# One decode step of attention plus an MLP mixer: TensorE's whole program in loops, V always in one home of SBUF

## The chip, the cores and the metric

The kernel runs on one core of a Trainium2 chip. A core has five engines with instruction streams of their own: PE (TensorE, matrix products into PSUM), DVE (VectorE), ACT (ScalarE), POOL (GpSimd) and SP (SyncE, which here issues nearly all loads). Each engine has a sequencer that reads instructions, works out addresses held in registers, takes branches, waits on semaphores, and hands the rest to its engine; PE's sequencer is called PEldq or PEq in the profile. Sixteen DMA engines move data between HBM and the on-chip memory SBUF. The metric is the device time in microseconds (us) of one execution; lower is better.

## What is computed

Two branches work on one token x of 1024 values, and their results are added. The attention has 32 query heads on 4 heads of K and V, with 65,536 cached keys of 128 values each: 64 MB of K and 64 MB of V in bf16.

```python
def _A_ref(x, k_cache, v_cache, wq, wo):          # Hq 32, Hkv 4, Sk 65536, Dh 128
    q = (x @ wq).reshape(B, Sq, Hq, Dh)            # transposed to b h s d
    scores = einsum("bhqd,bhkd->bhqk", q, k) * Dh ** -0.5
    o = einsum("bhqk,bhkd->bhqd", softmax(scores), v)
    return o.reshape(B, Sq, Hq * Dh) @ wo

def _B_ref(x, w1, w2, w3, w4):                     # S = 1, D 1024, F 3584
    h = gelu(layernorm(x) @ w1)
    # four quarters of h are shifted by 1, -1, 2, -2 tokens, with zeros let in
    x1 = x + shifted(h) @ w2
    return x1 + gelu(layernorm(x1) @ w3) @ w4

xn = layernorm(A_x)
return A_x + _A_ref(xn, ...) + _B_ref(xn, ...)
```

With one token, every shifted value is a zero that was let in, so the product with w2 adds nothing, though both kernels still load w1 and w2 and multiply by them.

## The kernel before

**Tiles.** Each head of K and V is cut into two tiles of 32,768 keys (r = 0 and 1), so there are 8 tiles (g, r), each with a K load and a V load of 8.39 MB. A tile of K or V fills a whole slot; there are three slots in SBUF, and the weights pass through the same slots. The list `items` (L193 to L201) is the order of the loads: wq, K(0,0), V(0,0), w3, K(0,1), V(0,1), wa (w1 and half of w4), then K and V in turn, wb (the rest of w4, and w2) ahead of the last V, and wo. Item i goes into slot i mod 3, and wo into the slot of the last K (L208, L209).

**Order.** Nothing schedules the work: the class `Flow` (L22) keeps for every buffer who wrote and read it, and puts a `wait_ge` on an engine's queue ahead of the instruction that needs it. Each engine runs in the order of the text. SP's loads are issued by `load` (L211): item i + 3 after the work on item i has been written down (L571), so a load waits on SP until the last user of its slot is done, and all later loads wait behind it.

**A tile of K** (`compute_K`, L442): DVE transposes the slot in place in four quarters (L449). PE multiplies each quarter by the queries into the scores `sc` in PSUM, in a hardware loop (`Fori`, L452) over the four banks; for most tiles the loop's body takes two quarters, 8 matmuls (CGS = 2), for the last tile one quarter, 4 matmuls (n_cg, L443). Its first matmul starts the accumulation. DVE takes the maximum (L462), two small transpositions on PE and two small steps on DVE give the common maximum (L463 to L469), ACT exponentiates all scores into `work` (L471), and DVE transposes `work` (L473).

**A tile of V** (`compute_V`, L495): 64 matmuls, written out one by one, four column groups side by side (L503). For r = 0 ACT copies the result to `ob` (L509), for r = 1 `group_end` (L513) adds both halves on DVE, and one matmul and four small DVE steps bring the group's output into `oT`.

**Weights.** `rows_product` (L314) multiplies the token by wq, w3 and w1, with the output row in four pieces on four column groups of PE at once. `rows_loop` (L328) does w4, w2 and the first 10 rows of wo with hardware loops; the other pieces of wo are written out (L536) and end the kernel, before a copy (L560) and the output's DMA.

Of the kernel before, what the change touches and what calls it, by code (L numbers as in the profile page):

```python
# [16 lines left out]
WO_PIECES = (10, 10, 8, 3, 1)  # L17
WO_UNROLL = 5
CGS = 2


class Flow:  # L22


    def __init__(self, nc, ctx):
        self.nc = nc
        self.ctx = ctx
        self.engines = {"T": nc.tensor, "V": nc.vector, "S": nc.scalar, "G": nc.gpsimd, "Q": nc.sync}
        self.sems = {}
        self.counts = {}  # L30
        self.seen = {e: {} for e in self.engines}
        self.writer = {}
        self.readers = {}

    def sem(self, name):
        if name not in self.sems:
            self.sems[name] = self.ctx.enter_context(self.nc.semaphore(f"s_{name}"))
            self.counts[name] = 0
        return self.sems[name]

    def _wait(self, eng, reads, writes):
# [7 lines left out]
        for key in reads:  # L49
            if key in self.writer:  # L50
                token = self.writer[key]
                if token[0] != "T" or eng != "T":
                    add(token)
        for key in writes:
            if key in self.writer:
                token = self.writer[key]
                if token[0] != "T" or eng != "T":
                    add(token)
            for token in self.readers.get(key, ()):
                if token[0] != eng:  # L60
                    add(token)
        for name, value in need.items():
            if self.seen[eng].get(name, 0) < value:
                self.engines[eng].wait_ge(self.sem(name), value)
                self.seen[eng][name] = value
# [8 lines left out]
    def op(self, eng, reads, writes, emit, times=1):  # L74

        self._wait(eng, reads, writes)
        sem = self.sem(eng)

        def signal(ins):
            ins.then_inc(sem, 1)  # L80

        emit(signal)
        self.counts[eng] += times
        self._note((eng, self.counts[eng]), reads, writes)
# [7 lines left out]

    def one(self, eng, reads, writes, call):
        self.op(eng, reads, writes, lambda signal: signal(call(self.engines[eng])))
# [3 lines left out]
def kernel(  # L98
# [28 lines left out]
    assert S == 1 and DH == P and REP == 8 and HQ == 32 and DC == 8 and NOUT == 1024  # L127
# [4 lines left out]
    FW = F // 8  # L132
    assert FW <= 512 and F % 8 == 0 and FW % 16 == 0 and FW // 16 == FC and OC == 32
    NQ = NOUT // 4
    NH = NOUT // 2
    FH = FC // 2
# [9 lines left out]
    slots = [tile_sb([P, KEYS], BF16, f"slot{i}") for i in range(SLOTS)]  # L146
    work = tile_sb([P, HF * 512], BF16, "work")
    ob = tile_sb([P, 512], F32, "ob")
    xpad = tile_sb([P, DC, 32], BF16, "xpad")
    QS = P + 24  # L150
    qst = [tile_sb([P, 4, QS], BF16, f"qst{i}") for i in range(2)]
    qsel = tile_sb([P, 4, HQ], BF16, "qsel")
    ident_bf = tile_sb([P, P], BF16, "ident_bf")
    ident_f = tile_sb([P, P], F32, "ident_f")
    og = tile_sb([P, P + 1], F32, "og")
    msk = tile_sb([P, 4, 32], F32, "msk")
    hstrip = tile_sb([P, 192], BF16, "hstrip")
    gsel = tile_sb([P, P], BF16, "gsel")
    sel32 = tile_sb([P, 32], F32, "sel32")
    sel8 = tile_sb([P, 8], F32, "sel8")  # L160
    sel8x = tile_sb([P, 32], F32, "sel8x")
    mask16 = tile_sb([P, 16], F32, "mask16")
    mask64 = tile_sb([P, 64], F32, "mask64")
# [3 lines left out]
    lnb = tile_sb([P, 8, DC], F32, "lnb")  # L167
    x_bf = tile_sb([P, DC], BF16, "x_bf")
    xn2b = tile_sb([P, DC], BF16, "xn2b")
    qT = tile_sb([P, HQ], BF16, "qT")  # L170
    hf_f = tile_sb([P, FC], F32, "hf_f")
    hT = tile_sb([P, FC], BF16, "hT")
    gT = tile_sb([P, DC], BF16, "gT")
    o5 = tile_sb([P, 32], F32, "o5")
    oT = tile_sb([P, OC], BF16, "oT")
    rep = msk[0:1].rearrange("p a b -> p (a b)")

    sc = ps.tile([P, HF, 512], F32, name="sc")
    oacc = ps.tile([P, 512], F32, name="oacc")
    pm = ps.tile([P, 512], F32, name="pm")  # L180
    psR = ps.tile([P, 2, 512], F32, name="psR")
    psB = sc[:, 0, :]
# [7 lines left out]
    assert sum(WO_PIECES) == OC  # L190
    wo_start = [sum(WO_PIECES[:i]) for i in range(len(WO_PIECES))]

    items = [("wq",), ("K", 0, 0), ("V", 0, 0), ("w3",)]  # L193
    for g in range(HKV):
        for r in range(NT):
            if (g, r) != (0, 0):
                items += [("K", g, r), ("V", g, r)]
            if (g, r) == (0, 1):
                items += [("wa",)]
    items.insert(len(items) - 1, ("wb",))  # L200
    items += [("wo",)]  # L201
# [4 lines left out]
    one, op = fl.one, fl.op  # L206

    slot_of = [i % SLOTS for i in range(len(items))]  # L208
    slot_of[-1] = slot_of[items.index(("K", HKV - 1, NT - 1))]  # L209

    def load(i):  # L211
        item, s = items[i], slot_of[i]
        t, kind = slots[s], items[i][0]
# [4 lines left out]
        elif kind == "wa":  # L218
            loads = [(0, w1_v), (KEYS // 2, w4_v[:, 0:FH * NOUT])]
        elif kind == "wb":  # L220
            loads = [(0, w4_v[:, FH * NOUT:FC * NOUT]), (KEYS // 2, w2_v)]
# [3 lines left out]
        else:  # L225
            cache = A_k_cache if kind == "K" else A_v_cache
            _, g, r = item
            loads = [(0, cache[0, g, r * KEYS:(r + 1) * KEYS, :].rearrange("(p k) d -> p (k d)", p=P))]
        fl._wait("Q", [], [("slot", s), ("slot", s, 1)] + [("slot", s, q) for q in range(2, 5)] + [("kt", s, cg) for cg in range(4)])
        for n, (at, src) in enumerate(loads):  # L230
            key = ("slot", s) if n == 0 else ("slot", s, n)
            fl.dma("Q", f"slot{s}" if n == 0 else f"slot{s}_{n}", [], [key], t[:, at:at + src.shape[-1]], src)

    qrow = work[:, 0:1024].rearrange("p (b n) -> p b n", b=2)
    psel = work[:, 1024:1536].rearrange("p (b m) -> p b m", b=4)
    ones_f = og[:, 0:P]
    xr = work[:, 1536:2048]

    load(0)
    fl.dma("S", "x", [], ["x_bf"], x_bf[:], A_x[0, 0, :].rearrange("(p c) -> p c", c=DC))  # L240
    load(1)
    load(2)
    one("G", [], ["xr"], lambda e: e.memset(xr[0:33, :], 0.0))
    fl.dma("S", "x2", [], ["xr"], xr[0:33:32, :], A_x[0, 0, :].rearrange("(j n) -> j n", j=2))

    def ident(t, key):
        one("G", [], [key], lambda e: e.memset(t[:], 0.0))
        one("G", [key], [key], lambda e: e.affine_select(
            out=t[:], in_=t[:], compare_op=ALU.not_equal, fill=1.0, base=0, pattern=[[-1, P]],
            channel_multiplier=1))  # L250

    eps_t, negmean, rstd, ln_s1, ln_s2 = (sm[:, i:i + 1] for i in range(5))
    ident(ident_bf, "ident_bf")
    ident(ident_f, "ident_f")
    one("G", [], ["eps"], lambda e: e.memset(eps_t, LN_EPS))
    one("G", [], ["ones"], lambda e: e.memset(ones_f, 1.0))
    one("G", [], ["xpad"], lambda e: e.memset(xpad[:], 0.0))
    one("G", [], [("qst", 0)], lambda e: e.memset(qst[0][:], 0.0))
    one("G", [], [("qst", 1)], lambda e: e.memset(qst[1][:], 0.0))
    one("G", [], ["hstrip"], lambda e: e.memset(hstrip[:], 0.0))  # L260

    def v(reads, writes, call):
        one("V", reads, writes, call)

    v(["ident_f"], ["sel32"], lambda e: e.tensor_tensor(out=sel32[:], in0=ident_f[:, 0:32], in1=ident_f[:, 32:64], op=ALU.add))
    v(["ident_f", "sel32"], ["sel32"], lambda e: e.tensor_tensor(out=sel32[:], in0=sel32[:], in1=ident_f[:, 64:96], op=ALU.add))
    v(["ident_f", "sel32"], ["sel32"], lambda e: e.tensor_tensor(out=sel32[:], in0=sel32[:], in1=ident_f[:, 96:128], op=ALU.add))
    v(["sel32"], ["mask16"], lambda e: e.tensor_tensor(out=mask16[:], in0=sel32[:, 0:16], in1=sel32[:, 16:32], op=ALU.add))
    v(["ident_f"], ["mask64"], lambda e: e.tensor_tensor(out=mask64[:], in0=ident_f[:, 0:64], in1=ident_f[:, 64:128], op=ALU.add))
    v(["sel32"], ["dmask"], lambda e: e.reduce_sum(out=dmask[:], in_=sel32[:].rearrange("p (cg h) -> p cg h", h=8), axis=AX.X))  # L270
    v(["sel32"], ["mask4"], lambda e: e.reduce_sum(out=mask4[:], in_=sel32[:].rearrange("p (x dd) -> p dd x", dd=4), axis=AX.X))
    v(["sel32"], ["sel8"], lambda e: e.reduce_sum(out=sel8[:], in_=sel32[:].rearrange("p (cg h) -> p h cg", h=8), axis=AX.X))
    v(["sel8"], ["sel8x"], lambda e: e.tensor_copy(out=sel8x[:].rearrange("p (h dd) -> p h dd", dd=4),
                                                   in_=sel8[:].unsqueeze(2).to_broadcast([P, 8, 4])))
    iv = ident_bf[:].rearrange("p (b i r) -> p b r i", b=2, r=2)
    for b in range(2):
        for par in range(2):
            v(["ident_bf"], [("psel", b, par)], lambda e: e.tensor_copy(
                out=psel[:, 2 * b + par, :].rearrange("p (a i) -> p a i", a=4),
                in_=iv[:, b, par, :].unsqueeze(1).to_broadcast([P, 4, 32])))  # L280
    psel_keys = [("psel", b, par) for b in range(2) for par in range(2)]
    lead = ident_bf[:].rearrange("p (j u) -> p j u", u=32)[:, :, 0]
    v(["ident_bf", "hstrip"], ["hstrip"], lambda e: e.tensor_copy(
# [322 lines left out]
```

## Time and profile before

| what | value |
|---|---|
| median of 3 runs | 402.4 us (402.27 to 402.55) |
| the profiled execution's own time | 402.23 us |
| its span, first to last instruction | 400.1 us |
| PE busy, DVE busy, ACT busy | 223.5, 210.5, 30.9 us |
| bytes read from HBM | 169.87 MB, 425 GB/s over the span |
| matmuls run | 1407 |

In the profile, lines such as L455 are those of the kernel above. In a group's line, `out<-in` names the buffers; `[.. <-X]` is the engine's idle time just before and what ended it. A timeline line starts with the start time and the duration in us. A busy engine that nothing waits for costs no time: what counts is which wait ends last.

### The profile page before, as it was taken

Reading aid. Unit: us, or ns where it says so; the run is one execution under the profiler, and the core shown is the slowest. Engines: PE = TensorE matmul, PEld = TensorE weight load, DVE = VectorE, ACT = ScalarE, POOL = GpSimd, SP = SyncE. Lnnn points to the kernel's source line nnn. Section 1 sums busy time; section 2 is a strip of 40 time slices with the busy share of each in tenths; the row PEclk is TensorE's granted clock in tenths of the full one; section 3 lists DMA queues with packets and bytes.
Section 4 is the critical chain, followed back from the end, with each engine's and each line's share of the span. In section 5 each row is a group of like instructions: output and inputs, shape, how many; then the busy total and the mean of one; then the engine's idle time right before and its main releaser. Section 6 shows DMA issues by size and latency. Waiting matters only on the chain.

```text
span 400.1 us, 4118 instructions
## 1 busy us (share of the span) xinstructions
PE 223.5 (56%) x1407; PEld 91.3 (23%) x1407; DVE 210.5 (53%) x191; ACT 30.9 (8%) x36; POOL 6.3 (2%) x28
## 2 busy tenths in 40 slices
PE   0263087360195563964395608845925194596985
PEld 0220033130042220421142203312402041232332
DVE  2201792210962448822972499269455963794421
ACT  1000000320001300003001000020020002000200
POOL 3000000000000000000000000000000000000000
PEclk9995579585589598795699567968988599799799
DMA  8999999999989999999999999999999999999995
GB/s 347 465 446 419 420 414 454 391 473 452 426 382 471 451 426 414 426 432 432 465 434 426 419 426 439 426 472 428 426 419 434 439 419 459 398 454 434 397 432 208
DMA packets 4054, 170.02 MB, mean 425 GB/s; under 512 B 582, under 2 KB 588, under 8 KB 844
## 3 DMA queue, kind: packets, MB, share of 16 engines
q1 hardware_dynamic: 3896, 169.87, 98.3%
q8 instruction: 8, 0.13, 0.1%
q10 hardware_dynamic: 148, 0.00, 0.0%
q14 instruction: 2, 0.02, 0.0%
HBM read 169.87 MB, written 0.00 MB: 425 GB/s over the span
## 4 chain that ended last, share of the span: by engine, by line
DMA 53%; PE 28%; DVE 13%; issue 4%; ACT 1%; SPq 1%; POOL 0%; ACTq 0%
DMA slot<-in_A_k_cache_dram 46%; PE sc L455 20%; DVE slot L449 10%; DMA slot<-in_A_wo_dram 7%; PE oacc L503 5%; PE psR L337 2%; DVE sm L462 2%; DVE work L473 1%; ACT work L471 1%; SPq L89 1%; PE sc L321 0%; DVE og L515 0%; ACT L471 0%; DVE sm L464 0%; PE pm L463 0%
## 5 line engine op out<-in xcount | busy, mean ns | idle before, releaser
L455 PE MATMUL sc<-slot,qst 128*128 x512 | 127.8, 407 | 77.4 <-DVE slot L449 76.4
L449 DVE STREAM_TRANSPOSE slot<-slot 128x4096 f32<-128x4096 f32 x32 | 139.4, 4413 | 29.7 <-DMA slot<-in_A_k_cache_dram 29.7
L455 PEld LDWEIGHTS sc<-slot,qst 128*128 128x128 bf16 x512 | 51.8, 101 | 154.2 <-issue 106.8
L503 PE MATMUL oacc<-slot,work 128*32 128x512 bf16 x512 | 45.7, 530 | 37.5 <-DVE work L473 21.9
L462 DVE TENSOR_REDUCE sm<-sc 128x1 f32<-128x2048 f32 x8 | 18.3, 2291 | 58.4 <-PE sc L455 58.4
L503 PEld LDWEIGHTS oacc<-slot,work 128*32 128x32 bf16 x512 | 19.0, 127 | 60.8 <-issue 56.9
L473 DVE STREAM_TRANSPOSE work<-work 128x2048 bf16<-128x2048 bf16 x8 | 18.5, 2312 | 21.2 <-ACT work L471 21.2
L471 ACT ACTIVATE work<-sc,sm 128x2048 bf16<-128x2048 f32 x8 | 15.7, 1967 | 147.1 <-DVE sm L469 147.1
L337 PE MATMUL psR<-slot,hT 128*1 x56 | 16.2, 438 | 0.5 <-issue 0.2
L515 DVE SCALAR_TENSOR_TENSOR og<-oacc,sm,og 128x128 f32<-128x128 f32 x16 | 5.6, 351 | 18.6 <-PE oacc L503 18.2
L321 PE MATMUL sc<-slot,xpad 128*32 128x512 bf16 (+1 forms) x144 | 11.1, 441 | 4.3 <-DMA slot<-in_A_wq_dram 4.3
L471 ACT ACT_TABLE_LOAD x3 | 3.8, 1283 | 117.5 <-DVE sm L469 117.5
L463 PE MATMUL pm<-ident_f,sm 128*1 128x128 f32 x8 | 2.2, 270 | 19.1 <-DVE sm L462 19.1
L294 PE MATMUL pm<-sm,og 128*128 128x1 f32 x4 | 1.2, 363 | 14.9 <-DVE sm L293 14.9
L337 PEld LDWEIGHTS psR<-slot,hT 128*1 x56 | 5.1, 92 | 10.9 <-issue 7.8
L321 PEld LDWEIGHTS sc<-slot,xpad 128*32 128x32 bf16 x144 | 5.4, 113 | 9.0 <-DMA slot<-in_A_wq_dram 4.4
L399 DVE TENSOR_TENSOR work<-pm,mask 128x448 f32<-128x448 f32 x1 | 0.6, 624 | 11.0 <-PE pm L394 11.0
L463 PEld LDWEIGHTS pm<-ident_f,sm 128*1 128x1 f32 x8 | 0.6, 79 | 23.0 <-DVE sm L462 23.0
L352 DVE CAST work<-sc 128x512 bf16<-128x512 f32 x1 | 0.7, 690 | 9.2 <-PE sc L321 9.2
L347 POOL COPY qst<-qsel 32x32 bf16<-32x32 bf16 x12 | 2.5, 206 | 189.0 <-PE sc L455 161.8
L337 PE MATMUL psR<-slot,oT 128*1 x20 | 4.5, 379 | 1.6 <-DVE oT L529 1.6
L509 ACT COPY ob<-oacc 128x512 f32<-128x512 f32 x4 | 2.3, 585 | 33.1 <-PE oacc L503 33.1
(99 smaller groups left out, 71.6 us busy)
## 6 DMA issues: line engine op xcount, KB each, us to landing
slot<-in_B_w_dram SPq DMA_DIRECT2D x1, 7168.0 KB, 50.8
slot<-in_B_w_dram SPq DMA_DIRECT2D x2, 3584.0 KB, 31.9
slot<-in_A_wo_dram SPq DMA_DIRECT2D x2, 2560.0 KB, 19.5
slot<-in_B_w_dram SPq DMA_DIRECT2D x2, 2048.0 KB, 30.1
slot<-in_A_wo_dram SPq DMA_DIRECT2D x1, 2048.0 KB, 26.7
slot<-in_A_wo_dram SPq DMA_DIRECT2D x1, 768.0 KB, 28.1
slot<-in_A_wo_dram SPq DMA_DIRECT2D x1, 256.0 KB, 28.4
slot<-in_A_k_cache_dram SPq DMA_DIRECT2D x8, 36.1
```

The costliest lines, as they stand in the source:

```text
L89: self.engines[eng].dma_start(out=out, in_=in_).then_inc(sem, 16)
L321: ins = nc.tensor.matmul(sc[32 * j:32 * j + 32, bk, 0:width], lhsT=xpad[:, c, :], rhs=wt[:, c, ch * width:(ch + 1) * width], start=(c == 0 ...
L337: ins = nc.tensor.matmul(psR[0:1, h, :], lhsT=lv[:, bass.ds(c, 1), u], rhs=wv[:, bass.ds(c, 1), u, h, :], start=False, stop=False, skip_gr ...
L347: lambda e: e.tensor_copy(out=qst[g % 2][sl, :, 24 + 32 * a:24 + 32 * a + 8], in_=qsel[sl, :, 8 * g:8 * g + 8]))
L449: v([("slot", s)], [("kt", s, cg)], lambda e: e.transpose(out=kf[:, cg, :], in_=kf[:, cg, :]))
L455: ins = nc.tensor.matmul(sc[:, bass.ds(hf, 1), :], lhsT=qst[g % 2][:, bp, 24 - 8 * cg:24 - 8 * cg + P], rhs=kr[:, cg, bass.ds(hf, 1), :, b ...
L462: v(["sc"], ["mx"], lambda e: e.reduce_max(out=mx, in_=sc[:].rearrange("p h n -> p (h n)"), axis=AX.X))
L463: one("T", ["mx", "ident_f"], ["pm"], lambda e: e.transpose(pm[0:1, 0:P], mx, ident_f[:]))
L471: one("S", ["sc", ("nball", r)], WORK + [("lall", r)], lambda e: e.activation(out=pT, in_=sc[:], func=ACTF.Exp, bias=nball[:, r:r + 1], sc ...
L473: v(["work"], ["work"], lambda e: e.transpose(out=pT, in_=pT))
L503: ins = nc.tensor.matmul(oacc[32 * u:32 * (u + 1), :], lhsT=pT[:, hf, 32 * t:32 * (t + 1)], rhs=vt[:, :, hf, t, :], start=(hf == 0 and t < 4),
L515: v(["oacc", ("wm", 1), "og"], ["og"], lambda e: e.scalar_tensor_tensor(out=og[:, 0:P], in0=oacc[:, P * cg:P * (cg + 1)], scalar=wm[:, 1, ...
```

## The change

TensorE's instructions are no longer written by `Flow` piece by piece. A function `tensor_program` writes them once, as loops: over wq and w3 (one loop of two turns), over the 4 groups, the 2 tiles and the 4 quarters, over the banks, over w4 and wo. Before, the built program has 939 matmul instructions for TensorE, after it 138. So that a loop's turns can all be the same:

- TensorE waits for tokens that it counts down: DVE, POOL and ACT raise `VT`, `GT` and `RT`, and `take` waits for one and subtracts it.
- The three slots are one tensor `home`. V always lies in part 0, K(g, r) in part 1 + r; wq, w3 and wa come first into parts 1, 0 and 2. The order of the loads is wq, w3, wa (w1, w2 and 13 rows of w4), then K and V in turn, wb (w4's last 15 rows, 9 and 6) behind the last V, and wo in seven pieces. The last K comes in two halves. After the work on tile t's PV has been written down, SP issues V(t+1) and K(t+2).
- The scores are added onto zeros that ACT writes into `sc` after each exponential. One loop body has 4 matmuls of one quarter and one bank, with the weights' address in registers too.
- The products with wq and w3 put one output row of 512 values after the other on partition 0 (64 matmuls each, the last 8 of w3 on zeros); ACT and DVE copy the row, and 32 small matmuls turn it into columns.
- The norms of x are worked out on one row by ACT, instead of on 128 partitions by DVE.
- w2's 8 rows and w4's first 13 are one loop; w4's last 15 and wo's first 24 another, after the last group's output.

```diff
-    def op(self, eng, reads, writes, emit, times=1):
...
+    def one(self, eng, reads, writes, call, tok=None, peek=()):
+        self._wait(eng, list(reads) + list(peek), writes)
+        if tok:
+            call(self.engines[eng]).then_inc(self.sem(tok), 1)
+            self._note(("tok", 0), [], writes)
+            return
...
+    items = [("wq",), ("w3",), ("wa",)]
     for g in range(HKV):
         for r in range(NT):
+            items += [("K", g, r), ("V", g, r)]
+    items += [("wb",), ("wo",)]
...
+    place = {"wq": 1, "w3": 0, "wa": 2, "V": 0, "wb": 1, "wo": 2}
+    slot_of = [1 + item[2] if item[0] == "K" else place[item[0]] for item in items]
...
+    def take(name, n=1):
+        te.wait_ge(tokens[name], n)
+        te.sem_inc(tokens[name], -n)
+
+    def tensor_program():
...
+        with te.Fori(0, 2) as i:
+            take("VT")
+            take("GT")
+            with te.Fori(0, 8) as ch:
+                for c in range(DC):
+                    ins = te.matmul(banks[0:1, bass.ds(ch, 1), :], lhsT=xn[:, bass.ds(i, 1), c],
+                                    rhs=home[:, bass.ds(i * (c * (F - NQ_ROW) - KEYS) + ch * 512 + KEYS + c * NQ_ROW, 512)],
+                                    start=(c == 0), stop=(c == DC - 1), skip_group_check=True)
+                ins.then_inc(sig, 1)
+            take("RT", 2)
+            with te.Fori(0, 8) as b:
+                for u in range(4):
+                    ins = te.matmul(pm[:, bass.ds(b * 4 + u, 1)], lhsT=row[:, bass.ds(b * 512 + u * P, P)],
+                                    rhs=ident_bf[0:1, 0:1], start=True, stop=True, skip_group_check=True)
+                ins.then_inc(sig, 1)
...
+        with te.Fori(0, HKV) as g:
+            with te.Fori(0, NT) as r:
+                with te.Fori(0, 4) as cg:
+                    take("VT")
+                    with te.Fori(0, HF) as hf:
+                        for bp in range(4):
+                            ins = te.matmul(sc[:, bass.ds(hf, 1), :],
+                                            lhsT=qst[:, bass.ds(g % 2, 1), bp, bass.ds(24 - cg * 8, P)],
+                                            rhs=kv[:, bass.ds(r * 16 + cg * 4 + hf + 16, 1), :, bp // 2, :, bp % 2],
+                                            start=False, stop=False, skip_group_check=True)
+                        ins.then_inc(sig, 1)
+                take("VT")
+                te.transpose(pm[0:1, 0:P], sm[:, 50:51], ident_f[:]).then_inc(sig, 1)
+                take("VT")
+                te.transpose(pm[:, P:P + 1], rep[0:1, :], ident_f[0:1, 0:1]).then_inc(sig, 1)
+                take("VT")
+                for y in range(64):
...
+        rows_loop(cols[:, DC + W4A:DC + W4A + n], home[:, so * KEYS - (FC - W4A) * NOUT:so * KEYS + WO_LOOP * NOUT], n, UNROLL,
+                  lambda: take("GT"))
...
+        for cg in range(4):
+            piece = cg // 2 if (g, r) == last_K[1:] else 0
+            v([], [("kt", ks, cg)], lambda e: e.transpose(out=kf[:, cg, :], in_=kf[:, cg, :]), tok="VT",
+              peek=[("slot", ks, piece), "sc", ("qst", g % 2)])
+            fl.pe([("kt", ks, cg), ("qst", g % 2)], ["sc"], HF)
...
+        v(["work"], ["work"], lambda e: e.transpose(out=workv, in_=workv), tok="VT", peek=[("slot", vs, 0), "oacc"])
+        fl.pe(["work", ("slot", vs, 0)], ["oacc"])
+        if not last:
+            s(["sm0"], ["sc"], lambda e: e.copy(out=sc, in_=zero.unsqueeze(2).to_broadcast([P, HF, 512])))
+            for n in (i + 3, i + 4):
+                if n < len(items) - 1:
+                    load(n)
```

In the changed kernel the loop over the scores' matmuls stands at L311 to L317, PV at L323 to L326, wq's and w3's passes at L263 to L268, the turning of a row at L270 to L274, w1 at L284, and the loops over rows at L293.

## The prediction

> **What bounds the kernel now.** The DMA row and the queue rows of the page were read first.
>
> ```profile
> DMA  8999999999989999999999999999999999999995
> ...
> q1 hardware_dynamic: 3896, 169.87, 98.3%
> q8 instruction: 8, 0.13, 0.1%
> ```
>
> The 16 DMA engines are busy from first slice to last: 169.87 MB have to come in, and nothing but their number sets the 400.1 us. Packet by packet, a 64 KB packet takes 2.418 us, so a K or V tile (8 packets an engine) streams in 19.35 us, and K lands every 38.7 us (DVE's waits for K end at 189.91 and 267.13, two tiles apart). Compute hides behind that only while SP can issue the next load before the last runs dry. So the second view is the timelines of DVE and SP around one tile, (2, 1), whose K landed at 267.13:
>
> ```profile
> 267.13 17.43 DVE L449 STREAM_TRANSPOSE slot<-slot 128x4096 f32<-128x4096 f32 x4 [0.89 <-DMA slot<-in_A_k_cache_dram]
> 292.12 2.29 DVE L462 TENSOR_REDUCE sm<-sc 128x1 f32<-128x2048 f32 x1 [7.55 <-PE sc L455]
> ...
> 297.94 2.31 DVE L473 STREAM_TRANSPOSE work<-work 128x2048 bf16<-128x2048 bf16 x1 [2.17 <-ACT work L471]
> ...
> 305.85 1.51 DVE L515 SCALAR_TENSOR_TENSOR og<-oacc,sm,og 128x128 f32<-128x128 f32 x4 [3.41 <-PE oacc L503]
> ```
>
> ```profile
> 292.17 0.33 SPq L89 DMA_DIRECT2D slot<-in_A_v_cache_dram  x1
> 305.89 0.33 SPq L89 DMA_DIRECT2D slot<-in_A_k_cache_dram  x1
> ```
>
> The tile needs 25.0 us from landing to the end of its scores (292.09) and 13.7 us more to the end of PV (305.83). The next V load goes out at the end of the scores, and only the K load behind it waits for PV; that leaves SP ten and more us in hand.
>
> Third, how fast TensorE runs a loop. These are matmul rows of tile (1, 1), whose loop body has 8 matmuls, and of the last tile, whose body has 4:
>
> ```profile
> 207.69 7.13 PE L455 MATMUL sc<-slot,qst 128*128 x32 [0.26 <-issue]
> ...
> 349.20 4.07 PE L455 MATMUL sc<-slot,qst 128*128 x16 [1.96 <-DVE slot L449]
> 353.53 12.82 PE L455 MATMUL sc<-slot,qst 128*128 x48 [0.26 <-issue]
> ```
>
> 8 a body: 223 ns each, near the 216 ns of back-to-back starts. 4 a body: 254 and 267 ns. What the short body waits for is PE's sequencer (PEldq: min/median/max in ns):
>
> ```profile
> L452 PEldq FUSED_REGOPS  x72: 78/78/83, 51.2 to 365.1; - x72
> L452 PEldq ALU_OP  x72: 32/36/36, 52.6 to 365.7; - x72
> L452 PEldq COMPARE_BRANCH  x72: 76/215/230, 52.7 to 365.9; - x72
> L452 PEldq MOVE  x18: 29/29/33, 51.2 to 361.9; - x18
> ```
>
> ```profile
> L455 PEldq FUSED_REGOPS  x480: 42/46/51, 51.5 to 365.6; - x160
> ```
>
> From start to start in the records: a head FUSED_REGOPS with six results (78 ns) 0.137 us; one with two results (42) 0.092; one with three (46) and the weight load and matmul behind it 0.124; one with six behind which a matmul goes (79, in L337's rows) 0.157; a weight load and matmul alone 0.032; ALU_OP 0.092; a branch taken (215) 0.274, not taken (83) 0.14; MOVE (29) 0.087; a semaphore wait (51) 0.1. L337's old body of 4 matmuls adds up to 1.03 us and ran in 1.04 to 1.12.
>
> **The change, part by part.** *Scores.* The loop is now one body of 4 matmuls, 4 times a quarter, 4 quarters a tile, with the weights' address dynamic too. The built body has four address words and a MOVE ahead of its first matmul (7, 6, 2, 4 results; those of 7 and 4 I put at 0.14 and 0.10 between their neighbours): 0.14 + 0.137 + 0.10 + 0.087 + 0.10 + 0.032 + 3 x 0.157 + 0.092 + 0.274 = 1.43 us, against 0.86 us of matmuls. Four of them, the last branch not taken: 5.60. Around them ALU, branch, two MOVEs and the token's wait: 0.64. A quarter is 6.24 us, a tile 25.0 from the first quarter's token, where DVE delivers a quarter every 4.36. TensorE's sequencer becomes the bound of the scores: landing to scores' end is 4.4 + 0.1 + 25.0 = 29.5 us where it was 25.0, or 22.0 in the last tile's form. Bounds of a quarter: 4.8 (last tile's 4.28 and half a us around it, the new words free) and 7.0 (10% over the sum, beyond L337's worst).
>
> *Scores to PV's end*: 8.3 us as now, PV at its mean of 5.9 (rows from 4.97 to 6.56), 0.2 for three token waits: 14.4. ACT's zeroing of sc (about 2.0 us, as L471's 1.97) lies beside DVE's 2.31 us transposition of work; without that cover it would be 2 us a tile.
>
> *Homes.* V(t+1) now waits for PV(t), and K(t+2) stands behind it in SP's queue. From PV's end, 1.1 us to the first packet (0.95 to 2.02 at the start), 38.7 of stream, 0.45 to the semaphore: K(t+2) lands 40.2 us after PV(t).
>
> *Pair of tiles.* r=0 to 1: DVE starts the next K 6.0 us before PV ends, its first token comes 1.5 before; PV end to PV end 25.0 - 1.5 + 14.4 = 37.9. r=1 to 0: DVE first does the group's end, 2.8 us (3.2 at 229.64 to 232.84, less the cast that is gone), then 4.5 to the token: 46.7. A pair is 84.6 us; K's landing needs 40.2 of 40.7, just not later. Loads alone need 77.4.
>
> *Start.* wq and w3 go through one output row, 8 passes of 8 matmuls with two address words each: 0.14 + 0.125 + 0.032 + 7 x 0.261 + 0.366 = 2.49 us a pass, 19.9 a matrix (5.86 and 3.2 now, four columns at once); turning a row to columns 8 x 1.10 = 8.8, twice; w1 6.0; w2 and w4's first rows 7 x 1.31 = 9.2. In order: wq lands 23.05, its product 43.6, copied (2.3 for 2048 values, as L462's row) 46.0, columns 55.1, w3 75.4, Gelu (2 x 1.8 by L390) 79.2, columns 88.0, q selected 88.8, w1 94.8, rows 104.3. K(0,0) has then lain there since 77; K(0,1) goes out at 104.4, 8 us after the stream ran dry, and V(0,1) only after PV(0,0): 104.3 + 25.0 + 14.4 + 1.3 (table load) = 145.0, another hole of 20 us. Before, these products ran between tiles while K and V came in. The norms on one row of ACT (four passes over 1024 values, about 1.1 each by L471's 1.97 for 2048, two roots, two table loads of 1.3, small steps: some 11 us from x's landing, 13.4 before) end at about 24 at worst, beside wq's load; without that cover they would add their 11.
>
> *End.* Last PV at 145.0 + 3 x 84.6 + 37.9 = 436.7. Then group end 2.0, 13 bodies of rows with a token at 1.50 = 19.5 (wo has landed by then), fold 1.3 and 0.6, last rows 0.5, copy 0.7, output 2.7: 464.
>
> SP's extra issues (wa in three pieces, the last K in two, w4 in two, wo in seven, 0.33 to 0.43 us each) stand behind loads of 4 us and more and cost nothing; were the stream dry, 0.4 each.
>
> *Instruction fetches* fall from 8 of 16 KB. Packet by packet, each holds one DMA engine 1.4 us, and engines with one end at 395.5 to 396.2, those without at 394.4: worth up to 1.7 us, and nothing while loads wait for compute.
>
> The profiled execution took 402.23 us with a span of 400.1 (median of the runs 402.4), 2.1 outside it. So 466. Bodies ran 1 to 9% over their steps' sum in L337 and up to 6% in the last scores; 4% on all of TensorE's loops is 12 us. I take half: **472 us**.
>
> [...]
>
> **Rivals.** [...]
>
> *C, the new address words hide.* A quarter at 4.8: scores 19.2, first PV 139; then K's landing rules, 40.2 + 4.5 + 19.2 + 14.4 = 78.3 a pair, last PV about 405, end 27: 435. For: the four words differ little from the old head. Against: every such word has its own time in L455's records.
>
> *D, the other side: the sequencer runs ahead.* If the words ahead of the queue cost nothing, the 4 matmuls keep 216 ns, DVE paces the scores, PV ends some 36 us after landing and the first packet of V follows at 37.2 of 38.2: DMA never dries. The decisive point is a quarter below about 4.4 us. Then the fetches' 1.7 us come off: 401. For: 8-matmul bodies do hide theirs. Against: the last tile's 4-matmul body did not.
>
> **How the numbers follow.** A 0.74, B 0.10, C 0.10, D 0.06. The time is A's, 472. Its own spread from quarters of 5.8 to 6.8 us (8 tiles, 4 quarters, 0.4 to 0.6 each) and the start is 450 to 490, B lies inside, C and D are left out with A's edges: 450 to 490. What a measurement here can tell from no change is 0.2%, 0.8 us. Faster is most of D, 0.04; same 0.02; slower 0.94.
>
> **What would show it.** Right: starts of L313's bodies 1.4 to 1.5 us apart, quarters of 6.2 to 6.6, wq's product 20 us long, DMA holes before K(0,1) and V(0,1), PV ends 38 and 47 us apart in turn. [...] Wrong: matmuls of L313 at 220 ns in rows of 16, or a DMA row of nines.

## The result, and the profile after

The changed kernel takes 612.45 us (611.11 to 613.71, four runs) against 402.33 us for the kernel before: ratio 1.5227, 95% interval 1.5194 to 1.526. The direction was forecast, the size was not: 472 us, 450 to 490, was written down. The profiled execution has a span of 608.9 us.

First the page of the changed kernel: two rows of the 40 slices, the queues, and two of the costliest groups (busy time, mean ns | idle time before them and what ended it).

```profile
PEclk9997785976786766767887676867777777767789
DMA  9999939390059909960897399319946990585850
...
q1 hardware_dynamic: 4472, 169.87, 65.7%
...
q8 instruction: 1, 0.02, 0.0%
...
L313 PE MATMUL banks<-home,qst 128*128 x512 | 176.3, 505 | 163.3 <-PEq L255 152.0
L519 DVE STREAM_TRANSPOSE home<-home 128x4096 f32<-128x4096 f32 x32 | 142.0, 4439 | 179.5 <-PE banks L313 171.6
```

The row of nines has holes: the same bytes flow for 65.7% of the span where it was 98.3%. The last line is the finding. DVE's transposition of a quarter of K now stands idle 171.6 us until PE's score matmuls are done. In the kernel before it waited for nothing but its DMA, 29.7 us in all:

```profile
L449 DVE STREAM_TRANSPOSE slot<-slot 128x4096 f32<-128x4096 f32 x32 | 139.4, 4413 | 29.7 <-DMA slot<-in_A_k_cache_dram 29.7
```

The timeline of DVE over the first tile of the changed kernel shows each of these waits:

```profile
110.55 4.45 DVE L519 STREAM_TRANSPOSE home<-home 128x4096 f32<-128x4096 f32 x1 [7.91 <-ACT banks L472]
124.04 4.45 DVE L519 STREAM_TRANSPOSE home<-home 128x4096 f32<-128x4096 f32 x1 [9.04 <-PE banks L313]
135.31 4.45 DVE L519 STREAM_TRANSPOSE home<-home 128x4096 f32<-128x4096 f32 x1 [6.83 <-PE banks L313]
147.07 4.45 DVE L519 STREAM_TRANSPOSE home<-home 128x4096 f32<-128x4096 f32 x1 [7.31 <-PE banks L313]
158.33 2.29 DVE L525 TENSOR_REDUCE sm<-banks 128x1 f32<-128x2048 f32 x1 [6.82 <-PE banks L313]
```

Before, the same four transpositions were one row of 17.43 us. Now DVE and PE take turns. A quarter has a median period of 11.3 us (from the matmuls' starts): 4.45 of DVE, 1.0 to PE's first matmul, 5.4 to the start of its last, 0.4 until DVE goes on. From the first transposition's start to the scores' end it is not 29.5 us, as forecast, but 47.8 in this tile and 45.6 to 46.0 in the next three. The wait has a place in the code: `peek` at L520 asks for "sc", the score banks, ahead of every transposition, and `fl.pe([...], ["sc"], HF)` names PE as the writer of these banks after each quarter. Only the first quarter of a tile needs it, because ACT zeroes the banks there; for the other three it waits for the matmuls just queued.

PE's bodies of 4 matmuls in that tile, and two of SP's issues of V, each at a PV's end:

```profile
118.19 1.04 PE L313 MATMUL banks<-home,qst 128*128 x4 [1.02 <-PEq L255]
119.77 1.04 PE L313 MATMUL banks<-home,qst 128*128 x4 [0.54 <-issue]
121.37 1.04 PE L313 MATMUL banks<-home,qst 128*128 x4 [0.55 <-issue]
122.96 1.04 PE L313 MATMUL banks<-home,qst 128*128 x4 [0.55 <-issue]
```

```profile
174.41 0.33 SPq L96 DMA_DIRECT2D home<-in_A_v_cache_dram  x1
...
228.84 0.33 SPq L96 DMA_DIRECT2D home<-in_A_v_cache_dram  x1
```

A body takes 1.59 us (1.43 forecast). The later issues of V are at 291.44, 345.73, 409.66, 462.25 and 525.84 us: PV ends lie 52.6 to 54.4 and 62.6 to 63.9 us apart in turn, where 37.9 and 46.7 were forecast.

From the packets of q1, the span can be split into the packets' own time (a mean over the 16 engines) and the rest, in which an engine has none:

```
kernel                                     span   packets   idle
before                                    400.1     393.5    6.6
after                                     608.9     400.3  208.6
DVE ahead                                 498.6     400.2   98.4
DVE ahead, bodies of 16                   445.9     398.4   47.5
the same, start written out               411.4     397.2   14.2
```

So of the 209 us more, 202 are idle time and 7 are slower packets. Of the idle time, some 185 us are ten holes ahead of loads that were issued late (the longest, 36.7 us, ahead of V(0,1) at 175.38), and most of the rest is an end that takes longer: 21.5 us from the last packet of wo to the end of the span, where it was 3.9.

### The profile page after: what moved, and what is told of

Read it like the earlier page. It is cut to its first block, busy times and chain, and to the rows that moved or that the text cites. A ratio compares the mean times of both kernels' runs of the same rounds, so it can differ in the third digit from the quotient of the medians.

```text
span 608.9 us, 5420 instructions
## 1 busy us (share of the span) xinstructions
PE 320.3 (53%) x1422; PEld 110.3 (18%) x1422; DVE 209.0 (34%) x157; ACT 52.7 (9%) x51; POOL 7.3 (1%) x33
## 3 DMA queue, kind: packets, MB, share of 16 engines
q1 hardware_dynamic: 4472, 169.87, 65.7%
HBM read 169.87 MB, written 0.00 MB: 279 GB/s over the span
## 5 line engine op out<-in xcount | busy, mean ns | idle before, releaser
L313 PE MATMUL banks<-home,qst 128*128 x512 | 176.3, 505 | 163.3 <-PEq L255 152.0
L519 DVE STREAM_TRANSPOSE home<-home 128x4096 f32<-128x4096 f32 x32 | 142.0, 4439 | 179.5 <-PE banks L313 171.6
L313 PEld LDWEIGHTS banks<-home,qst 128*128 x512 | 58.1, 114 | 280.7 <-issue 261.5
L325 PE MATMUL banks<-home,scratch 128*32 128x512 bf16 x512 | 48.3, 559 | 40.0 <-PEq L255 40.0
L265 PE MATMUL banks<-home,xn 128*1 x128 | 43.2, 413 | 19.7 <-PEq L255 15.7
L533 ACT ACTIVATE scratch<-banks,sm 128x2048 bf16<-128x2048 f32 x8 | 15.7, 1967 | 346.2 <-DVE sm L532 346.1
L525 DVE TENSOR_REDUCE sm<-banks 128x1 f32<-128x2048 f32 x8 | 18.3, 2292 | 55.1 <-PE banks L313 55.1
L325 PEld LDWEIGHTS banks<-home,scratch 128*32 128x32 bf16 x512 | 19.8, 133 | 65.1 <-issue 63.2
L297 PE MATMUL banks<-home,cols 128*1 x120 | 29.1, 395 | 1.4 <-PEq L255 0.5
L535 DVE STREAM_TRANSPOSE scratch<-scratch 128x2048 bf16<-128x2048 bf16 x8 | 18.5, 2311 | 18.8 <-ACT scratch L533 18.8
L272 PE MATMUL banks<-ident_bf,scratch 1*128 1x1 bf16 x64 | 10.3, 178 | 13.0 <-PEq L255 6.6
L297 PEld LDWEIGHTS banks<-home,cols 128*1 x120 | 10.2, 85 | 20.0 <-issue 10.1
## 6 DMA issues: line engine op xcount, KB each, us to landing
home<-in_A_wo_dram SPq DMA_DIRECT2D x4, 1536.0 KB, 11.3
```

The costliest lines, as they stand in the source:

```text
L265: ins = te.matmul(banks[0:1, bass.ds(ch, 1), :], lhsT=xn[:, bass.ds(i, 1), c], rhs=home[:, bass.ds(i * (c * (F - NQ_ROW) - KEYS) + ch * 51 ...
L272: ins = te.matmul(pm[:, bass.ds(b * 4 + u, 1)], lhsT=row[:, bass.ds(b * 512 + u * P, P)], rhs=ident_bf[0:1, 0:1], start=True, stop=True, s ...
L297: ins = te.matmul(psR[0:1, h, :], lhsT=lv[:, bass.ds(c, 1), u], rhs=wv[:, bass.ds(c, 1), u, h, :], start=False, stop=False, skip_group_che ...
L313: ins = te.matmul(sc[:, bass.ds(hf, 1), :], lhsT=qst[:, bass.ds(g % 2, 1), bp, bass.ds(24 - cg * 8, P)], rhs=kv[:, bass.ds(r * 16 + cg * 4 ...
L325: ins = te.matmul(oacc[32 * u:32 * (u + 1), :], lhsT=work[:, 32 * y:32 * (y + 1)], rhs=vt[:, :, y, :], start=(y < 4), stop=(y >= 60), tile ...
L519: v([], [("kt", ks, cg)], lambda e: e.transpose(out=kf[:, cg, :], in_=kf[:, cg, :]), tok="VT", peek=[("slot", ks, piece), "sc", ("qst", g ...
```

## The experiments

All are edits of the changed kernel or of the one before. Where no interval is given, the time is one execution; the kernel before took 402.2 to 402.9 us beside them.

**1. DVE ahead** (500.62 us). The wait for the score banks is kept for the first quarter alone.

```diff
-              peek=[("slot", ks, piece), "sc", ("qst", g % 2)])
+              peek=[("slot", ks, piece), ("qst", g % 2)] + (["sc"] if cg == 0 else []))
```

> The changed kernel, except that DVE waits for the score banks to be zeroed only ahead of a tile's first transposition, so it may run ahead of TensorE. Theory (turn-taking: in the changed kernel each quarter's transposition, 4.45 us, stands behind the 16 matmuls of the quarter before it, because it asks for the banks that those matmuls wrote): the quarter falls from 11.6 us to what TensorE's sequencer needs, 4 x 1.595 + 0.5 = 6.9, the scores of a tile from 47.8 us to about 33, eight tiles give back 8 x 14.8 = 118 us: about 494 us, 485 to 510. Rival (the loop words of the sequencer alone make the quarter 11.6, the wait hides beside them): 590 to 612 us.

One condition gives back 112 us. The timeline of DVE in tile (1, 1):

```profile
243.96 17.42 DVE L519 STREAM_TRANSPOSE home<-home 128x4096 f32<-128x4096 f32 x4 [0.36 <-DMA home<-in_A_k_cache_dram]
276.00 2.29 DVE L525 TENSOR_REDUCE sm<-banks 128x1 f32<-128x2048 f32 x1 [14.62 <-PE banks L313]
```

The four transpositions are one row again, and the wait of 14.62 us stands behind them: PE is now the slower one, with a median quarter of 6.92 us. The rival, that the sequencer alone makes the quarter (590 to 612 us), is out.

**2. Bodies of 16, DVE's wait kept** (566.19 us), and **3. both edits** (447.98 us).

```diff
-                    with te.Fori(0, HF) as hf:
+                    for hf in range(HF):
                         for bp in range(4):
-                            ins = te.matmul(sc[:, bass.ds(hf, 1), :],
+                            ins = te.matmul(sc[:, hf:hf + 1, :],
```

> The changed kernel with the loop over a quarter's four parts written out: one body of 16 matmuls instead of four bodies of 4; DVE's wait stays. Turn-taking theory: a quarter is 4.45 of DVE, about 1.0 of hand-over and 16 matmuls in about 4.2 us, 9.7 in place of 11.6, so 4 x 1.9 x 8 = 61 us come off: about 552 us, 540 to 565. Rival (sequencer alone): the quarter falls to about 4.8 and the time to 450 to 480 us.

> Both edits: DVE may run ahead, and the body has 16 matmuls. Theory: the quarter falls to 4.5 to 4.8 us, the pace of DVE's transpositions; then the landing of K, two tiles after a PV, sets a pair at about 78 us (40.2 + 4.5 + 19.2 + 14.4) and the start and the end are left as they are: about 453 us, 443 to 470. If the two edits were worth the sum of what each brings alone to the changed kernel, without that new bound, it would be about 612 - 118 - 61 = 433.

Alone the edits bring 112 and 46 us, together 164. With both, DVE waits for the landing of K again (tile (1, 1) of the third kernel):

```profile
228.34 17.42 DVE L519 STREAM_TRANSPOSE home<-home 128x4096 f32<-128x4096 f32 x4 [8.34 <-DMA home<-in_A_k_cache_dram]
250.20 2.29 DVE L525 TENSOR_REDUCE sm<-banks 128x1 f32<-128x2048 f32 x1 [4.44 <-PE banks L313]
```

Its pairs of PV ends from the first on are 78.2, 79.2 and 78.5 us, as expected (78). Experiment 2 came out 14 us over its 552 and 1 us above its range: its quarter is 10.3 us, not 9.7. Two windows of its second group say why (PE, PEld, DVE, ACT and POOL busy with counts, granted clock, DMA share, GB/s):

```profile
236.60:238.60 2.00, 2.00 (x6) 0.73 (x6) 0.00 (x0) 0.00 (x0) 0.00 (x0) 0.50 0.76 328
...
240.60:241.60 1.00, 0.97 (x5) 0.23 (x3) 0.00 (x0) 0.00 (x0) 0.00 (x0) 1.00 1.96 852
```

PE had been idle for 5.24 us and started at half its clock: 16 matmuls took 4.65 us from first start to last (median), against 3.28 in experiment 3.

**4. The turn-taking put into the kernel before** (492.28 us).

```diff
-CGS = 2
+CGS = 1
...
-                v([("slot", s)], [("kt", s, cg)], lambda e: ...)
+                v([("slot", s)] + (["sc"] if cp and (g, r) != (HKV - 1, NT - 1) else []), [("kt", s, cg)], lambda e: ...)
```

> The kernel before with the turn-taking put in: quarters one by one (bodies of 4 matmuls in its old loop), and each transposition after the first waits for the matmuls of the quarter before it, in all tiles but the last. Its loops, homes, start and end stay. Theory: a quarter is 4.45 + 1.0 + 4.3 = 9.7, landing to scores' end 39 us instead of 25.0; with 13.7 to PV's end less some 7 of overlap a tile takes about 46 to 49, more than its 38.7 us of loads, so seven tiles cost 50 to 70 us: 450 to 475 us. Rival (the ten us that SP has in hand swallow it): 402 to 415 us.

The edit puts in the wait and, with it, the old loop's body of 4 matmuls (CGS = 1). Together they cost 89 us, with the old homes and start; the ten us in hand don't hold it. That it is the wait and not the short body shows in the same run: its last tile has the short body and no wait, and ends its scores 21.9 us after the first transposition's start, where the tile with the waits ahead of it takes 40.9 (387.30 to 428.17):

```profile
418.00 4.45 DVE L449 STREAM_TRANSPOSE slot<-slot 128x4096 f32<-128x4096 f32 x1 [5.73 <-PE sc L455]
428.17 2.29 DVE L462 TENSOR_REDUCE sm<-sc 128x1 f32<-128x2048 f32 x1 [5.72 <-PE sc L455]
...
436.37 17.38 DVE L449 STREAM_TRANSPOSE slot<-slot 128x4096 f32<-128x4096 f32 x4
458.25 2.29 DVE L462 TENSOR_REDUCE sm<-sc 128x1 f32<-128x2048 f32 x1 [4.50 <-PE sc L455]
```

The time is 17 us above the range. A quarter took 10.2 us instead of 9.7: as in experiment 2, 16 matmuls behind some 5 us of rest were slow (4.95 us, median, where 4.3 had been expected). Over three quarters of seven tiles that is some 10 us of it, and the rest was not followed up.

**5. The start written out**, on top of experiment 3 (413.43 us), **and by itself** on the changed kernel (587.98 us).

```diff
-        with te.Fori(0, 2) as i:
+        for i in range(2):
...
-            with te.Fori(0, 8) as ch:
+            for ch in range(8):
...
-            with te.Fori(0, 8) as b:
+            for b in range(8):
```

> The changed kernel with DVE ahead and bodies of 16 (447.98 us), and its start written out: the 64 + 64 products with wq and w3 and the 32 + 32 one-column products without loops. Theory (most of what is left over the kernel before lies in the start, where the stream runs dry behind the two products at 3.0 us a pass): a pass of 8 matmuls falls to about 1.8 us, 9.5 us off each matrix, and the columns lose some 4 us each: 27 us off, about 421 us, 414 to 430. Rival (the homes and the end hold the rest): 438 us or more.

> The changed kernel with its start written out and nothing else. Theory (the terms add up: with DVE ahead and long bodies the written-out start ended the first PV 31.3 us earlier, 116.7 in place of 148.0; behind the start this kernel waits for turns, not for loads): 612.4 - 31 = 581 us, 575 to 587. Rival (the start lies beside work that is late anyway): over 595.

On top of experiment 3 it brings 34.5 us, with idle DMA time down from 47.5 to 14.2 us. By itself it ends the first PV 31.5 us earlier (142.90 against 174.41), as expected, but only 24.5 us are left at the end, and 587.98 lies just outside the 575 to 587: quarters take 11.67 us on average there against 11.36. The same body is slower in that program, though its four matmuls take 1.04 us there too, as in the changed kernel where 1.00 of the clock was granted (118 to 124 us):

```profile
85.44 1.04 PE L313 MATMUL banks<-home,qst 128*128 x4 [1.07 <-PEq L255]
87.11 1.04 PE L313 MATMUL banks<-home,qst 128*128 x4 [0.64 <-issue]
88.76 1.04 PE L313 MATMUL banks<-home,qst 128*128 x4 [0.61 <-issue]
```

Its starts are 1.65 to 1.67 us apart instead of 1.59. In the sequencer's records, from a quarter's second body on, the word behind the body's first address word comes mostly 0.31 us after it, where it was 0.23 in the changed kernel. Three times 0.08 us are most of the 0.31 us a quarter; why the same word takes longer there stays open.

**6. A filler for the clock** (539.97 us), on experiment 2: 16 matmuls behind each quarter whose result nobody reads.

```diff
+                    for _ in range(16):
+                        te.matmul(pm[:], lhsT=ident_bf[:], rhs=psel[:].rearrange("p b m -> p (b m)"), start=True, stop=True)
```

> The changed kernel with bodies of 16 and DVE's wait kept (566.19 us), and 16 more matmuls after every quarter whose result nobody reads (3.5 us at 216 ns), so that TensorE is not idle through DVE's next transposition. Theory (the idle time between the turns halves the granted clock, which is why 16 matmuls took 4.65 us from first start to last there and 3.27 us where DVE runs ahead): the clock stays at 1.0, a quarter falls from 10.3 to about 9.1 us, three quarters of eight tiles give back 29 us less about 8 us that the filler adds ahead of the maximum's transposition: about 545 us, 530 to 555. Rival (the 16 matmuls are slow for another reason, DVE's traffic or the words of the sequencer): the filler brings nothing and costs its 8 us: 566 to 580.

512 useless matmuls make the kernel 26 us faster. Tile (1, 0), whose line numbers are two higher:

```profile
223.31 4.45 DVE L521 STREAM_TRANSPOSE home<-home 128x4096 f32<-128x4096 f32 x1 [6.22 <-PE banks L313]
232.21 4.45 DVE L521 STREAM_TRANSPOSE home<-home 128x4096 f32<-128x4096 f32 x1 [4.46 <-PE banks L313]
241.08 4.45 DVE L521 STREAM_TRANSPOSE home<-home 128x4096 f32<-128x4096 f32 x1 [4.43 <-PE banks L313]
```

The first quarter behind PV and the group's end still finds PE slow (6.22 us of wait), the others do not (4.46); the clock granted from 225 to 233 us is 1.00, and 16 matmuls take 3.28 us (median).

**7. The homes alone**, in the kernel before. A first attempt (402.2 us) only moved the load in the program's text:

> The kernel before with the rule of the homes alone: from tile (1,0) on, the next V load goes out with the K load behind PV instead of at the end of the scores, five times. Theory (the stream runs dry for the 1.1 us from PV's end to the first packet and a little more each time): 1.5 to 2 us a tile, 402.9 + 5 x 1.75 = about 411 us, 406 to 418. Rival from the prediction's working (K(t+2) lands 40.2 us after PV(t) and the whole 13.7 us later issue of V counts): 5 x 3.7 us of lost hand and more, 421 or above; or nothing at all, 402 to 404.

Its trace shows V issued at 292.53 and K at 306.18 us, 13.7 apart as ever: SP runs on its own, and what holds a load is its wait, not its place in the text. That run says nothing of the homes. The second has the wait:

```diff
+            if len(held) > 1:
+                fl._wait("Q", ["oacc"], [])
+            for n in held:
+                load(n)
+            held = []
```

> The kernel before with the rule of the homes, this time with a wait: from tile (1,0) on, SP holds the next V load until PV has ended (in the run before, the load was only moved in the text of the program, and SP issued it at the scores' end as ever). Theory: what is queued at a K's landing streams for 38.7 us, and PV ends 38.7 us after that landing, so the stream runs dry for about the 1.1 us from issue to first packet at some of five turns: 0.5 to 1.4 us each, about 405.5 us, 403.5 to 409. Rivals: the hand that SP has swallows it, 402 to 402.8; the 13.7 us later issue counts whole, 412 or above.

418.83 us, ratio 1.0405 (1.0387 to 1.0424). The theory is refuted and the time is where the second rival put it (412 or above), though not for its reason: of the 13.7 us only a part is lost. Its SP timeline:

```profile
193.21 0.42 SPq L89 DMA_DIRECT2D slot<-in_A_k_cache_dram  x1
228.34 0.33 SPq L89 DMA_DIRECT2D slot<-in_A_v_cache_dram  x1
...
275.45 0.33 SPq L89 DMA_DIRECT2D slot<-in_A_v_cache_dram  x1
```

DVE's wait for the K issued at 193.21 ends at 235.20, 42.0 us later, and from there to PV's end (275.45, where the next V goes out) it is 40.3: two tiles take 82.2 us where their loads take 77.4. The holes are 4.0 to 5.6 us, one in a pair. So, as an estimate, the rule costs nothing as long as landing to PV's end is under some 77.4 - 42.0 = 35 us, and the kernel before needs 38.7 (25.0 to the scores' end and 13.7 more). With bodies of 16 the scores end 21.9 us after landing (experiment 3 above), which makes about 36, and in experiment 5 the packets show hardly 1 us of idle DMA between 120 us and 395 us.

**8. The changed kernel's order at the start**, in the kernel before (402.14 us).

```diff
-    items = [("wq",), ("K", 0, 0), ("V", 0, 0), ("w3",)]
+    items = [("wq",), ("w3",), ("wa",)]
```

> The kernel before with the changed kernel's order of loads and work at the start: wq, w3, w1/w4's first half, then all K and V; its own fast products (four columns at once, written out) and its own homes. Theory (it is the pace of the looped products and not the order that empties the stream): K(0,0) goes out at about 30 us, V(0,0) at 45, K(0,1) at 67 while loads until 92 are queued: no hole, 402 to 406 us. Rival (the order costs by itself, since nothing can be computed beside the weights): 412 us or more.

The order costs nothing; the pace of the looped products does, as experiment 5 shows from the other side. V(0,0) went out at 46.31 us and K(0,1) at 62.95, in the changed kernel at 86.57 and 117.24.

**9. Eight a body**, on experiment 1 (460.88 us): two banks a turn, loops kept.

> The changed kernel with DVE ahead (500.62 us) and two parts a body, 8 matmuls in place of 4, the loops kept. Theory (the time of a body is a fixed 0.97 us of address words and branch in the sequencer's records and 0.153 a matmul): 0.97 + 0.13 for one more address word + 8 x 0.153 = about 2.3 us a body, 5.1 a quarter in place of 6.9; a tile's scores lie below what the landing of K allows, so most of the way to the 447.98 us of 16 a body: about 453 us, 448 to 462. Rival (every matmul of such a loop costs its 0.4 us, however many stand in a body): a quarter stays at 6.5 or more, 490 to 500.

```profile
118.09 1.91 PE L314 MATMUL banks<-home,qst 128*128 x8 [1.04 <-PEq L255]
120.38 1.91 PE L314 MATMUL banks<-home,qst 128*128 x8 [0.37 <-issue]
```

A body is 2.29 us and a quarter 5.10, both as expected from the sequencer's records: by that estimate 0.97 of a body's 1.59 us don't depend on the number of its matmuls, and here twice as many share them.

**10. The end written out** too, on experiment 5: 411.05 us, 408.51 to 415.05 in four runs, ratio 1.0252 (1.02 to 1.0304).

> The kernel of DVE ahead, bodies of 16 and the start written out (413.43 us), with the loop of the end (13 bodies, w4's last 15 rows and 24 rows of wo) written out too. Theory (its bodies of 6 matmuls run at 1.57 us against 1.30 of matmuls and end at 405.3 where the last of wo has landed by about 402): 3 to 4 us come off, 410 us, 409 to 411.5, and what is left over the kernel before is 3.7 us that the smaller pieces of the loads take and the hole behind the first PV. Rival (the end waits for wo's pieces and not for the loop): 412.5 to 414.

In its profiled run (408.5 us) the rows of wo end at 400.8 instead of 405.7 us, and the last of them wait for pieces of wo. Three runs lie at 408.5 to 411.4 and one at 415.05, against a single run of 413.43, so what it brings is not settled. No version beat the kernel before, whose DMA idles only 6.6 us.

## Why the prediction was wrong

**The failed step** is in the scores: "a tile 25.0 from the first quarter's token, where DVE delivers a quarter every 4.36". The forecast took DVE's pace from the kernel before and let it run ahead of PE. It read the changed loop on PE's side, and on DVE's side only the transposition itself, not the list of what that transposition waits for; the "sc" in `peek` stood in the diff. Delivered was a quarter every 11.3 us. Experiment 1 prices the step: 612.45 - 500.62 = 112 us of the 140 us by which the forecast was off (118 us between experiments 2 and 3, with bodies of 16). No rival held it: each of them priced the words and branches of PE's sequencer, and none a wait on DVE's side.

**The rest of the forecast describes experiment 1**, the same program without that wait. 500.62 us is still above the range of 450 to 490, but there only sizes were off. 472 against 500.62 us:

- *Body of 4 matmuls:* 1.43 forecast, 1.593 measured at full clock. The two head words were put at 0.14 and 0.137 us from start to start; the records mostly have 0.23 (seven results, 173 ns busy) and 0.167 (109 ns). Their prices had been set by the number of results alone, from words that took 78 ns. A quarter is 6.92 and not 6.24, a pair 89.9 and not 84.6: three pairs, 16 us. The last tile adds 39.0 and not 37.9, 1 us.
- *Start:* rows end at 117.2, not 104.3. A pass of 8 matmuls took 3.0 us, not 2.49 (two matrices, 8 us), and the product's first matmul started at 26.80, not 23.05: it waits for the second small load of x (`x_bf`), which lands at 25.05, and that wait had been put at nothing beside wq's load. Columns (8.3 against 8.8), w1 (5.9 against 6.0) and rows (9.5 against 9.2) were right. First PV end 161.26 against 145.0, 16 us.
- *End:* 28.7 from the last PV's end against 27.3. The 6 us set aside for slow bodies come off again: 16 + 16 + 1 + 1 - 6 = 28, and 28.6 is the difference.

**Right:** that late issue, and not bytes, sets the time; the alternation of short and long gaps; 14.4 us from scores to PV's end (15.0, 13.9 and 14.3 in the changed kernel's second to fourth tile). "K's landing needs 40.2 of 40.7, just not later" was too tight: in experiment 3 DVE's wait for K(1,0) ends at 189.75, 41.8 us after PV(0,0) (148.00). In experiment 1 this hardly shows (DVE waits 0.36 us above) because its pairs are longer than forecast.

**Rivals.** B (0.10 in the forecast, inside its range), a dear back branch of the r loop, was the author's assumption, and the result refutes it: that branch takes 0.21 to 0.23 us when taken (L308), and q8 has 1 packet where it had 8. No run shows a fetch on this loop. C, words that hide, first PV at 139 and then K's landing: that is what experiment 3 makes (448 us, pairs of 78.5), but a longer body was needed for it. D, a stream that never dries, needed the start written out as well (experiment 5).

**Where 210 us went:** 164 to the turns and the short bodies (112 and 46 alone, the rest only together), 34.5 to the looped start, and the last 9 to 11 are the packets' own time (3 to 4), a hole of 2 to 3 us behind the first PV, and an end that comes later. The shares go by the order in which the edits were added: alone, the start is worth 24.5 us.

## What to carry to other kernels

Price a rewritten loop from both sides: for each instruction on the other engine, read the whole list of what it waits for, and ask who wrote that last by then; a wait that is right once per tile takes the overlap away when it is asked once per quarter. Take a word's price from a word that computes the same thing, and make a dynamic body long enough to share its fixed 0.97 us. Whether a load can be issued later for nothing has to be worked out for the pace at hand: the fixed home cost 16 us where landing to PV's end was 40 us, and about 1 us where the scores were quicker.

## What the hardware showed that was not expected

**Rest cost clock here.** In experiment 2 the turns left PE idle for 5.24 us, and it came back at a granted clock of 0.50 (236.60 to 238.60 us), with 1.00 again from 240.60 on. The filler of experiment 6 stands in that rest: 1.00 from 225 to 233 us, and 16 matmuls in 3.28 us (median) where experiment 2 took 4.65. How long a rest has to be was not measured. In the traces of before and after, score matmuls start 427 ns apart at 0.50 (median) and 216 to 218 ns at 1.00. In the changed kernel itself the clock counts for little: 281.9 us of its span are granted at 0.50, yet 16 matmuls take 5.43 us from first start to last (median) against 5.42 in experiment 1. Half clock needs 1.71 us for 4 matmuls (4 times 427 ns), hardly more than the 1.59 in which the sequencer feeds them; only the 8 quarters of 32 that lie 90% or more in it take longer, 5.8 to 6.2 us.

**The first packets behind a hole were slow.** In the changed kernel a 64 KB packet took 2.418 us (median), but up to 3.61 right behind a hole (at 229.91 us, where the hole ends at 229.79). What 64 KB packets took over 2.418 us adds up to 6.7 us an engine in the changed kernel and 1.0 in the kernel before, so that this is nearly all of the step from 393.5 to 400.3 us of packets for the same 169.87 MB.
